# One VectorE instruction for the row sums of an attention head: a column sum that transposes its input, in place of a 32 by 32 transposition and a sum

## The chip, the cores and the metric

The kernel runs on one core of a Trainium2 chip. The metric is the device time of one execution in microseconds (us), the median of several runs. The engines of the core are TensorE (PE in the profile; its weight loads are PEld), VectorE (DVE), ScalarE (ACT), GpSimd (POOL) and SyncE (SP), which issues the transfers.

## The reference

Block-causal attention for 8 batches of 8 heads (576 positions, 64 columns a head, blocks of 64), and behind it a gated MLP on all 4608 positions:

```python
scores = scale * np.matmul(q, k.transpose(0, 1, 3, 2))      # q, k, v: (8, 8, 576, 64)
mask = block_i >= block_j                                   # blocks of 64 positions
scores = np.where(mask, scores, -1000000000.0)
scores = scores - np.max(scores, axis=-1, keepdims=True)
attn = np.exp(scores)
attn = attn / (np.sum(attn, axis=-1, keepdims=True) + 1e-09)
x = np.matmul(attn, v)          # heads side by side: (4608, 512)
a = x @ w1                      # (512, 1024)
b = x @ w2
h = a * b @ w3                  # (1024, 1024)
out = h @ w_out                 # (1024, 512)
```

The change lies in `np.sum(attn, axis=-1)`.

## The kernel before, in words

The work is staged by pairs of heads, 32 of them (8 batches of 4 pairs), numbered n; j is the head of a pair. The scores are held transposed, keys on the 128 partitions (five chunks of 128 keys, the last of 64) and queries along the columns, so that the exponentials can go into the product with the values as they are. The sum over a row of the attention is then a sum over partitions and chunks.

The first four pairs run while the weights come in, and take their row sums in another way (a column of ones in the values; `take_early`). The change does not touch them. From the fifth pair on (about 170 us) each head goes as follows:

- `s_tile` (L235): products of q and k, each in two passes (`hi` and `lo` parts), into one of two PSUM tiles `s`. ScalarE takes the exponential twice, once in full precision into `p`, or into `rsum` for the first chunk (L250), and once rounded into `ph` (L251). VectorE makes the low part `pl` as the difference (L253). GpSimd adds the chunks of `p` into `rsum` (L256), a tile of 128 partitions by 576 queries.
- `pv` (L291): products of `ph` and `pl` with the values, into the PSUM tile `x`.
- `sums` (step R of the plan): `rsum` is transposed in blocks of 32 by 32 into `tr` (L304), and then each 32 columns of `tr` are added up (L305). The result, 18 columns a head, goes into `part`. Each of its numbers is the sum over one group of 32 partitions for one query.
- `take` (step N): ScalarE copies half of `x` to `xlow` (L323), VectorE adds the other half (L324).
- `total` (step T, once for both heads of a pair): a small product `tot` (L309) adds the four groups of partitions; VectorE adds 1e-9 (L311). `norm` takes the reciprocal (L327), spreads it by a transposition into `rb` (L329) and multiplies (L330). `finish_x` rounds to `xh` on ScalarE (L339) and makes the low part `xl` on GpSimd (L340).

For the next pair, the parts of q and k are prepared meanwhile: `hi` casts on VectorE (L160) with differences on GpSimd (L209, L212), `vs` for the values (cast on ScalarE, difference L225 on GpSimd), and the row maxima `m`: products `mx` (L182), maxima on VectorE (L186, L188), a transposition `mt` on TensorE (L190) and a copy on ScalarE (L192).

The MLP of the batch before is cut into small steps (F in the plan) that stand between those of the attention: products `ab` (L388) with copy `a` on ScalarE (L393), the gate `g` on VectorE (L395), `gh` on ScalarE (L396) and `gl` on GpSimd (L397), then products `o` (L404) with a copy (L408). After the last pair the MLP of the last batch runs alone.

The order of the work is set by a plan written out by hand, one letter a step, for the first and the second head of a pair:

```python
PLAN = (
    "B F B F S F S B F F S S F F F S M M V F V V V F R F F V Q N",
    "M A S S A F F S F M M S F F F S M A M V V V F V F F V N Q F R T M F F",
)
```

TensorE's order is this order as written. Every engine works through its own queue in order. A tile pool puts in the waits between engines.

Of the kernel before, what the change touches and what calls it, by code (L numbers as in the profile page):

```python
# [7 lines left out]
F32 = mybir.dt.float32  # L8
# [4 lines left out]
ALU = mybir.AluOpType  # L13
AX = mybir.AxisListType
PSUM = bass.MemoryType.PSUM

P = 128
B, H, S, D = 8, 8, 576, 64
BLK = 64
NB = S // BLK  # L20
NPAIR = H // 2
# [4 lines left out]
NF = DF // P  # L26
HALF = S // 2
RAW = 2 * S + 640
EARLY = NPAIR  # pairs whose work is spread over more engines while the weights come in
SCALE = 0.125  # L30
BIG = 8.0e9

# Columns of a head's probabilities (keys on partitions): a chunk of 128 keys
# takes the queries that may see it; zeros keep every product 256 columns wide.
PC = [128, 704, 1152, 1536, 1920]
PW = 1984
QLO = [0, 128, 256, 384, 512]
# The same without zeros, less the first query.
PE = [0, 448, 768, 960, 1024]


# Order of a head's steps, for the first and the second head of a pair.
PLAN = (
    "B F B F S F S B F F S S F F F S M M V F V V V F R F F V Q N",
    "M A S S A F F S F M M S F F F S M A M V V V F V F F V N Q F R T M F F",
)
# The same for the pairs before the first product of the MLP, while the weights come in.
EARLY_PLAN = (
    "M S S S C S C C C C M S V V B C M M V A V M V M Q B M A B M N",
    "S C C S A S S C S C V V V V V Q N T",  # L50
)
# Steps of the first pair with the MLP beside it that leave the MLP's place empty.
DELAY = 3
# Whether ScalarE makes the roundings of (q and k, q, k, k for the maxima, q for the maxima, v).
CAST = (0, 0, 1, 1, 1, 1)


# [1 line left out]
def block_causal_attention__then__gated_mlp_kernel(ctx, tc, qkv, consts, ident_in, w1, w2, w3t, wout, out_t):  # L59
    nc = tc.nc  # L60
# [4 lines left out]
    work = ctx.enter_context(tc.tile_pool(name="work", bufs=1))  # L65
# [6 lines left out]
    both = cpool.tile([P, 2 * P], F32, name="ident")  # L72
# [2 lines left out]
    w1l = cpool.tile([P, NC, DF], F32R, name="w1l")  # L75
    wh = cpool.tile([P, NF, DM], F32R, name="wh")
    wl = cpool.tile([P, NF, DM], F32R, name="wl")
    # Per head of a pair: (q, k) with high parts on the head's own half of the
    # partitions and q high, k low on the other; and (q low, k high) on the own
    # half with the rows that shift and mask the scores on the other.  # L80
    hi = [cpool.tile([P, 2, S], F32R, name=f"hi{j}") for j in range(2)]
    lo = [cpool.tile([P, 2, S], F32R, name=f"lo{j}") for j in range(2)]
    w2h = cpool.tile([P, NC, DF], F32R, name="w2h")
    w2l = cpool.tile([P, NC, DF], F32R, name="w2l")
    # Queries of both heads of a pair, block by block on a diagonal.
    qd = cpool.tile([P, NB, P], BF16, name="qd")
    own = [slice(0, D), slice(D, P)]
    oth = [slice(D, P), slice(0, D)]
# [12 lines left out]
    for j in range(2):  # L101
        nc.vector.tensor_copy(lo[j][oth[j]], cst[0:D, 0 : 2 * S].rearrange("p (t s) -> p t s", t=2))
    nc.gpsimd.memset(qd, 0.0)
    # Tiles of the time while the weights come in, and those that take their bytes.
    tl = {}

    def open_early(pool):
# [3 lines left out]
    def open_late():  # L111
        pool = ctx.enter_context(tc.tile_pool(name="late", bufs=1, reuse_waits="tile"))
        tl["late"] = pool
        tl["ph"] = pool.tile([P, PW], F32R, name="ph")
        tl["sum"] = pool.tile([P, S], F32, name="rsum")
        tl["pl"] = pool.tile([P, PW], F32R, name="pl")
        # Values: high part on the columns of the head's own half, low part on the other.
        tl["vs"] = [pool.tile([P, 5, P], F32R, name=f"vs{j}") for j in range(2)]
        for t in (tl["ph"], tl["pl"]):
            for a, b in ((0, PC[0]), (PC[2] + 320, PC[3]), (PC[3] + 192, PC[4])):  # L120
                nc.gpsimd.memset(t[:, a:b].bitcast(F32), 0.0)
        tl["gh"] = pool.tile([P, NF, HALF], F32R, name="gh")
        tl["gl"] = pool.tile([P, NF, HALF], F32R, name="gl")

    def load_w(dst, src, k):
        """512 columns of float64 words (low, high), as float32.

        Magnitudes below float32's smallest normal become zero.
        """
        t = tl["early"].tile([P, 1024], F32, tag="wraw", name="wraw", bufs=5)  # L130
        u = tl["early"].tile([P, 512], F32, tag="wbits", name="wbits", bufs=6)
        wide = t.bitcast(I32)
        nc.sync.dma_start(out=wide.rearrange("p (k w) -> p k w", k=k), in_=src)
        wide = wide.rearrange("p (c two) -> p c two", two=2)
        low, high = wide[:, :, 0], wide[:, :, 1]
        bits = u.bitcast(I32)
        V = nc.vector
        nc.scalar.activation(u, high.bitcast(F32), AF.Abs)
        V.tensor_scalar(out=u, in0=u, scalar1=2.0**-15, scalar2=None, op0=ALU.max)
        V.tensor_scalar(out=bits, in0=bits, scalar1=3, scalar2=0x3FFFFFF8, op0=ALU.logical_shift_left, op1=ALU.bitwise_and)  # L140
        V.scalar_tensor_tensor(out=bits, in0=high, scalar=-0x40000000, in1=bits, op0=ALU.bitwise_and, op1=ALU.bitwise_or)  # L141
        if dst is None:
            dst = u.unsqueeze(1)
        V.scalar_tensor_tensor(out=dst.bitcast(I32), in0=low.rearrange("p (k w) -> p k w", k=k), scalar=29,
                               in1=bits.rearrange("p (k w) -> p k w", k=k), op0=ALU.logical_shift_right, op1=ALU.bitwise_or)
        return u
# [115 lines left out]
        [(2, 256, 576, 256)],  # L262
        [(3, 320, 576, 384), (4, 512, 576, 512)],
    ]
    # (chunk, first column of the probabilities, width, first column in PSUM)
    PV = [(0, 0, 256, 256), (0, PC[0] + 128, 448, 512), (1, PC[1], 448, 512), (2, PC[2], 320, 640),
          (3, PC[3] - 64, 256, 704), (4, PC[4] - 192, 256, 704)]

# [30 lines left out]
    x_of = {}  # L299

    def sums(n, j, part):
        """Sums over the keys: 32 by 32 transposes, then over the groups of 32 partitions."""
        tr = work.tile([P, S], F32, tag="tr", name=f"tr{n}_{j}")
        nc.vector.transpose(tr, tl["sum"])  # L304
        nc.vector.reduce_sum(part[:, j, :], tr.rearrange("p (b c) -> p b c", c=32), axis=AX.X)  # L305

    def total(n, part, rr):
        tot = ps_q.tile([P, 512], F32, tag="psq", name=f"tot{n}")
# [117 lines left out]
    weights = gen_w(wp)  # L426

    def pair(n):
        """The attention of a pair of heads, with what the plan places between its steps."""
        early = n < EARLY  # L430
        x32 = work.tile([P, S], F32, tag="x32", name=f"x32_{n}")
        rr = work.tile([P, S // 32], F32, tag="rr", name=f"rr{n}")
        part = None if early else work.tile([P, 2, S // 32], F32, tag="part", name=f"part{n}")
        last = n + 1 == NN
        masks = iter(()) if last else shift_mask(n + 1)
        own_qk = prep_qk(n, 1)
        next_qk = iter(()) if last else prep_qk(n + 1, 0)
        for j in range(2):
            xps = ps_x.tile([P, 1024], F32, tag="psx", name=f"x{n}_{j}")
            p_early = wp.tile([P, 1600], F32, tag="pe", name=f"pe{n}_{j}") if early else None  # L440
            tiles = iter(S_TILES)
            pvs = (pv_early if early else pv)(n, j, xps, p_early)
            delay = DELAY if n == NPAIR and j == 0 else 0
            for step in (EARLY_PLAN if early else PLAN)[j].split():
                if step == "C":
                    fill(weights, 1)
                    continue
                with tc.high_priority(offset=0) if early else nullcontext():
                    if step == "S":
                        s_tile(n, j, next(tiles), p_early)  # L450
                    elif step == "F":
                        if delay:
                            delay -= 1
                        else:
                            fill(mlp, 1)
                    elif step == "M":
                        fill(masks, 1)
                    elif step == "A":
                        fill(next_qk, 1)
                    elif step == "B":  # L460
                        fill(own_qk, 1)
                    elif step == "V":
                        fill(pvs, 1)
                    elif step == "R":
                        sums(n, j, part)
                    elif step == "N" and early:
                        take_early(n, j, xps, x32, rr)
                    elif step == "N":
                        take(n, j, xps, x32)
                    elif step == "T":  # L470
                        if not early:
                            total(n, part, rr)
                        norm(n, x32, rr)
                        finish_x(n, x32)
                    elif step == "Q" and not last:
                        if n + 1 != NPAIR:
                            prep_v(n + 1, j)
                        if j == 1 and n + 2 < NN:
                            load(n + 2)
# [5 lines left out]
    open_late()  # L485
    for j in range(2):
        prep_v(NPAIR, j)
    # Products of the gated MLP stand between those of the attention, which wait for other engines.
    ctx.enter_context(tc.manual_schedule(engines={mybir.EngineType.PE}))
    mlp = (None for b in range(B - 1) for _ in gen_moe(b))  # L490
    for n in range(NPAIR, NN):
# [52 lines left out]
```

## Time and profile before

| what | value |
|---|---|
| median of 3 runs | 1069.15 us (1067.49 to 1069.55) |
| span of the profiled execution | 1066.6 us, 18267 instructions |
| the profiled execution's time beside its span | not given apart; the median of the runs lies 2.55 us above the span |
| TensorE busy | 986.9 us (93%) |
| VectorE busy | 810.3 us (76%), 1432 instructions |
| ScalarE busy | 594.9 us (56%) |
| GpSimd busy | 601.4 us (56%) |
| mean granted TensorE clock | 0.982 |

The profile is one execution, with times from the start of the span. Matmuls are pipelined and their ends are modelled, so that the busy time of TensorE says less than the distance from one start to the next. In a row of a timeline the first number is the start, the second how long it took, both in us; a bracket at its end gives how long the engine had been idle before it and what ended that. The letters L and a number are a line of the kernel.

### The profile page before, as it was taken

The numbers are of one execution on the slowest core, as the hardware profiler recorded it, in microseconds if no ns is written. First come the engines' busy times: TensorE is split into PE (matmuls) and PEld (weight loads), VectorE is DVE, ScalarE is ACT, GpSimd is POOL, SyncE is SP. The second block draws the span as 40 slices with busy tenths as digits, with TensorE's granted clock in tenths as the row PEclk, the third lists the DMA queues.
The fourth block names the chain that finished last, engine by engine and source line by source line (L and its number), as shares of the span: only waits on it lengthen the run. The fifth ranks groups of instructions, "written<-read, shape, count | busy, mean of one in ns | idle before, by whom it ended". The sixth has DMA issues, their size and how long they took to land.

```text
span 1066.6 us, 18267 instructions
## 1 busy us (share of the span) xinstructions
PE 986.9 (93%) x6624; PEld 892.7 (84%) x6624; DVE 810.3 (76%) x1432; ACT 594.9 (56%) x1505; POOL 601.4 (56%) x631
## 2 busy tenths in 40 slices
PE   3789778999999999999999999999999999999998
PEld 1444347999998989999999989899999999899998
DVE  7999997878787887778787888877787878886100
ACT  4646566656665656556565656565565656554221
POOL 3324367656575666666565756666665657564211
PEclk9889889999999999999999999999999999999999
DMA  6665421111111001111111110111111111000000
GB/s 214 202 194 191 140 73 36 35 58 36 58 35 54 18 34 47 41 52 36 58 36 58 36 47 19 39 47 42 52 36 58 35 59 36 22 3 18 7 24 23
DMA packets 27196, 61.52 MB, mean 58 GB/s; under 512 B 3361, under 2 KB 19873, under 8 KB 27105
## 3 DMA queue, kind: packets, MB, share of 16 engines
q1 hardware_dynamic: 27104, 60.35, 17.0%
q8 instruction: 52, 0.85, 0.3%
q14 instruction: 40, 0.32, 0.1%
HBM read 50.76 MB, written 9.44 MB: 56 GB/s over the span
## 4 chain that ended last, share of the span: by engine, by line
PE 47%; DVE 34%; ACT 11%; issue 6%; DMA 1%; POOL 1%; ACTq 0%; DVEq 0%; SPq 0%; POOLq 0%
PE ab L388 21%; PE o L404 12%; DVE pl L253 6%; PE s L235 6%; DVE m L186 4%; DVE hi L160 3%; DVE part L305 3%; DVE tr L304 3%; ACT ph L251 3%; DVE g L395 2%; PE x L291 2%; ACT p L250 2%; PE mx L182 2%; PE w L365 2%; DVE wbits L141 2%
## 5 line engine op out<-in xcount | busy, mean ns | idle before, releaser
L256 POOL TENSOR_TENSOR rsum<-rsum,p 128x448 f32<-128x448 f32 x224 | 176.7, 789 | 124.1 <-ACT p L250 116.6
L253 DVE TENSOR_TENSOR pl<-p,ph 128x448 fp32r<-128x448 f32 x168 | 149.1, 901 | 62.2 <-ACT ph L251 61.3
L397 POOL TENSOR_TENSOR gl<-g,gh 128x288 fp32r<-128x288 f32 x128 | 107.5, 840 | 138.0 <-ACT gh L396 135.6
L396 ACT CAST gh<-g 128x288 fp32r<-128x288 f32 x128 | 55.5, 433 | 228.2 <-DVE g L395 228.2
L235 PE MATMUL s<-hi 128*128 128x288 f32 (+4 forms) x384 | 127.8, 344 | 29.0 <-ACT ph L251 21.4
L388 PE MATMUL ab<-xh,w2h 128*128 128x288 f32 x512 | 153.3, 300 | 0.1
L404 PE MATMUL o<-gh,wh 128*128 128x288 f32 x512 | 152.1, 297 | 0.0
L388 PE MATMUL ab<-xh,w1h 128*128 128x288 f32 x512 | 150.9, 295 | 1.1 <-ACT xh L339 1.1
L388 PE MATMUL ab<-xl,w1h 128*128 128x288 f32 x512 | 151.0, 295 | 0.5 <-POOL xl L340 0.5
L388 PE MATMUL ab<-xh,w2l 128*128 128x288 f32 x512 | 150.9, 295 | 0.0
L388 PE MATMUL ab<-xh,w1l 128*128 128x288 f32 x512 | 150.9, 295 | 0.0
L388 PE MATMUL ab<-xl,w2h 128*128 128x288 f32 x512 | 150.9, 295 | 0.0
L404 PE MATMUL o<-gh,wl 128*128 128x288 f32 x512 | 150.8, 295 | 0.0
L404 PE MATMUL o<-gl,wh 128*128 128x288 f32 x512 | 150.7, 294 | 0.0
L186 DVE TENSOR_REDUCE m<-mx 128x1 f32<-128x512 f32 (+6 forms) x320 | 128.1, 446 | 5.0 <-PE mx L182 3.2
L251 ACT ACTIVATE ph<-s 128x288 fp32r<-128x288 f32 x336 | 131.3, 393 | 0.0
L209 POOL TENSOR_TENSOR hi<-raw,hi 64x576 fp32r<-64x576 f32 x64 | 93.7, 1464 | 43.2 <-ACT hi L160 17.8
L291 PE MATMUL x<-ph,vs 128*128 128x256 f32 x336 | 111.6, 340 | 0.1
L250 ACT ACTIVATE p<-s 128x448 f32<-128x448 f32 x224 | 85.4, 381 | 44.6 <-PE s L235 44.3
L235 PE MATMUL s<-lo 128*128 128x288 f32 (+4 forms) x384 | 107.0, 307 | 2.2 <-DMA lo<-ms 1.2
L235 PEld LDWEIGHTS s<-hi 128*128 128x128 f32 (+1 forms) x384 | 70.9, 185 | 45.5 <-ACT ph L251 28.0
L395 DVE TENSOR_TENSOR g<-ab,a 128x288 f32<-128x288 f32 x128 | 57.4, 448 | 66.4 <-PE ab L388 65.5
(77 smaller groups left out, 2558.7 us busy)
## 6 DMA issues: line engine op xcount, KB each, us to landing
raw<-in_qkv SPq DMA_DIRECT2D x32, 896.0 KB
out_t<-o SPq DMA_DIRECT2D x64, 144.0 KB
wraw<-in_w3t SPq DMA_DIRECT2D x16, 512.0 KB
wraw<-in_w SPq DMA_DIRECT2D x16, 512.0 KB
wraw<-in_wout SPq DMA_DIRECT2D x8, 512.0 KB
lo<-ms SPq DMA_DIRECT2D x64, 2.2 KB
cst<-in_consts SPq DMA_DIRECT2D x1, 288.0 KB
ident<-in_ident SPq DMA_DIRECT2D x1, 128.0 KB
```

Source lines behind the costliest of these rows:

```text
L186: nc.vector.reduce_max(m[:, col : col + 1], sc, axis=AX.X)
L209: nc.gpsimd.tensor_tensor(out=hi[j][x, 1, :], in0=rqk[o, 1, :], in1=hi[j][o, 1, :], op=ALU.subtract)
L235: nc.tensor.matmul(t[ks, at : at + q1 - q0], src[:, 1, kr], src[:, 0, q0:q1], start=(s == 0), stop=(s == 1))
L250: nc.scalar.activation(p32, t[ks, at : at + w], AF.Exp, scale=SCALE)
L251: nc.scalar.activation(ph[ks, o : o + w], t[ks, at : at + w], AF.Exp, scale=SCALE)
L253: nc.vector.tensor_tensor(out=low, in0=p32, in1=ph[ks, o : o + w], op=ALU.subtract)
L256: nc.gpsimd.tensor_tensor(out=r, in0=r, in1=p32, op=ALU.add)
L291: nc.tensor.matmul(xps[:, to : to + w], v[:, c, :], pr[:, a : a + w], start=(u < 2 and s == 0), stop=(u in (0, len(PV) - 1) and s == len(p ...
L388: nc.tensor.matmul(t[:, 0:HALF], l[:, c, fs], r, start=(c == 0 and s == 0), stop=(c == NC - 1 and s == 2))
L395: nc.vector.tensor_tensor(out=g32, in0=acc[1][:, 0:HALF], in1=a32, op=ALU.mult)
L397: nc.gpsimd.tensor_tensor(out=gl[:, f, :], in0=g32, in1=gh[:, f, :], op=ALU.subtract)
L404: nc.tensor.matmul(t[:, 0:HALF], l[:, f, es], r[:, f, :], start=(f == 0 and s == 0), stop=(f == NF - 1 and s == 2))
```

## The change

`sums` loses the transposition and the tile `tr`. The sum over each 32 columns reads `rsum` itself and is told to transpose its input in blocks of 32 by 32 (`apply_transpose=True`).

```diff
     def sums(n, j, part):
-        """Sums over the keys: 32 by 32 transposes, then over the groups of 32 partitions."""
-        tr = work.tile([P, S], F32, tag="tr", name=f"tr{n}_{j}")
-        nc.vector.transpose(tr, tl["sum"])
-        nc.vector.reduce_sum(part[:, j, :], tr.rearrange("p (b c) -> p b c", c=32), axis=AX.X)
+
+        blocks = tl["sum"].rearrange("p (b c) -> p b c", c=32)
+        nc.vector.tensor_reduce(part[:, j, :], blocks, axis=AX.X, op=ALU.add, apply_transpose=True)
```

The rest of the change takes out comments, so that lines behind L304 have a number less by one. The order of every other instruction on every engine is as before; on VectorE the new one stands where the transposition stood. Two places in VectorE's queue show it. The first is the sums of the first head of pair 6, `hi_84` being the cast for the next pair's first head, `m` the next pair's maxima and `g` the MLP's gate; before:

```order
L186 TENSOR_REDUCE m_2020<-mx_0_2021 128x1 [waits PE_49]
L304 STREAM_TRANSPOSE tr_0_2047<-rsum 128x576 [waits DVE_49,Pool_49]
L160 CAST hi_84<-raw_1854 64x576
L305 TENSOR_REDUCE part_1905<-tr_0_2047 128x18 [waits DVE_49]
L395 TENSOR_TENSOR g_2058<-ab,a_2056 128x288 [waits PE_49,Activation_49]
L186 TENSOR_REDUCE m_2020<-mx_1_2076 128x1 [waits PE_49]
```

After the change the cast is followed by the gate at once:

```order
L186 TENSOR_REDUCE m_2012<-mx_0_2013 128x1 [waits PE_49]
L304 TENSOR_REDUCE part_1897<-rsum 128x18 [waits Pool_49]
L160 CAST hi_84<-raw_1848 64x576
L394 TENSOR_TENSOR g_2048<-ab,a_2046 128x288 [waits PE_49,Activation_49]
L186 TENSOR_REDUCE m_2012<-mx_1_2066 128x1 [waits PE_49]
```

So `part` comes ahead of the cast instead of behind it, and `g` moves up one place. The second is the sums of the second head of pair 5, with `tot` and the normalisation behind them; before:

```order
L304 STREAM_TRANSPOSE tr_1_1862<-rsum 128x576 [waits DVE_49,Pool_49]
L188 TENSOR_TENSOR m_1649<-m_1649 128x1 [waits DVE_49]
L160 CAST hi_85<-raw_1475 64x576
L305 TENSOR_REDUCE part_1530<-tr_1_1862 128x18 [waits DVE_49]
L324 TENSOR_TENSOR x_5_1528<-x_1_1704,xlow_1_1849 64x576 [waits Activation_49]
L311 TENSOR_SCALAR rr_1529<-tot_1865 64x18 [waits PE_49]
```

After it:

```order
L304 TENSOR_REDUCE part_1526<-rsum 128x18 [waits Pool_49]
L188 TENSOR_TENSOR m_1645<-m_1645 128x1 [waits DVE_49]
L160 CAST hi_85<-raw_1473 64x576
L323 TENSOR_TENSOR x_5_1524<-x_1_1698,xlow_1_1843 64x576 [waits Activation_49]
L310 TENSOR_SCALAR rr_1525<-tot_1857 64x18 [waits PE_49]
```

Here `part` moves ahead of m and the cast, and x stands directly behind the cast.

## The prediction

> **What bounds the kernel now.** I read the stretches first, then the waits of TensorE, then the two tiles that the change touches, and last the timeline of two neighbouring pairs. The table by stretches cuts the span where the attention with the MLP beside it begins (170 us) and ends (985 us); its columns are the busy time of each engine with instruction counts, then the granted clock.
>
> ```profile
> core 0: us, PE busy (x) PEld busy (x) DVE busy (x) ACT busy (x) POOL busy (x), PEclk, DMA share, GB/s
> 170.00:985.00 815.00, 781.97 (x5643) 745.56 (x5643) 649.90 (x1160) 476.35 (x1271) 514.29 (x553) 1.00 0.12 40
> 985.00:1066.60 81.60, 78.42 (x592) 78.19 (x590) 8.09 (x18) 17.68 (x43) 14.48 (x18) 0.99 0.06 19
> ```
>
> TensorE is busy 96% of the middle stretch at full clock, VectorE 80%. All the changed instructions lie in that stretch, so VectorE time counts only where TensorE waits for it, directly or through another engine. The waits of TensorE there (us in total, times, longest):
>
> ```profile
> PE s L235 <- ACT ph L251: 21.4, 27, 0.8
> PE tot L309 <- DVE part L305: 7.7, 13, 0.6
> PE x L291 <- DVE pl L253: 3.6, 14, 0.3
> ```
>
> One is named after the changed instruction itself (L305), once in every second pair. The largest, 27 times, is named after ScalarE; the timeline shows what stands behind it. First the two instructions in question, from the view of the tile between them (min/median/max ns):
>
> ```profile
> L304 DVE STREAM_TRANSPOSE tr<-rsum x56: 765/768/778, 176.9 to 979.5; 128x576 f32<-128x576 f32 x56
> L305 DVE TENSOR_REDUCE part<-tr x56: 728/753/754, 178.5 to 980.4; 128x18 f32<-128x576 f32 x56
> ```
>
> They take 43 + 42 us of VectorE in 56 heads. Both are flat whatever GpSimd does beside them.
>
> **The first place: sums of a pair's first head (27 TensorE waits).** VectorE's, ScalarE's and TensorE's timelines in one pair (start, us):
>
> ```profile
> 411.24 0.69 DVE L186 TENSOR_REDUCE m<-mx 128x1 f32<-128x512 f32 x1
> 411.85 0.77 DVE L304 STREAM_TRANSPOSE tr<-rsum 128x576 f32<-128x576 f32 x1
> 412.64 0.70 DVE L160 CAST hi<-raw 64x576 fp32r<-64x576 f32 x1
> 413.38 0.75 DVE L305 TENSOR_REDUCE part<-tr 128x18 f32<-128x576 f32 x1
> 414.05 0.45 DVE L395 TENSOR_TENSOR g<-ab,a 128x288 f32<-128x288 f32 x1
> ```
> ```profile
> 414.53 0.43 ACT L396 CAST gh<-g 128x288 fp32r<-128x288 f32 x1 [3.45 <-DVE g L395]
> 414.87 0.46 ACT L160 CAST vs<-raw 128x320 fp32r<-128x320 f32 x1
> 415.35 0.64 ACT L323 COPY xlow<-x 64x576 f32<-64x576 f32 x1
> 416.01 0.41 ACT L250 ACTIVATE rsum<-s 128x288 f32<-128x288 f32 x1
> 416.31 0.41 ACT L251 ACTIVATE ph<-s 128x288 fp32r<-128x288 f32 x1
> ```
> ```profile
> 412.41 0.29 PE L388 MATMUL ab<-xl,w2h 128*128 128x288 f32 x1
> 413.34 0.28 PE L291 MATMUL x<-ph,vs 128*128 128x256 f32 x1
> 415.55 0.29 PE L388 MATMUL ab<-xh,w2l 128*128 128x288 f32 x1
> 415.68 0.29 PE L388 MATMUL ab<-xl,w2h 128*128 128x288 f32 x1
> 416.77 0.47 PE L235 MATMUL s<-hi 128*128 128x448 f32 x1 [0.80 <-ACT ph L251]
> ```
>
> VectorE stands in a queue without gaps: transpose, a cast, the sum, then g. ScalarE had been idle 3.45 us for g, then works without gaps to the ph that TensorE waits for. So the sum (L305) is on the path that ends the wait. Matmuls start 0.13 apart (415.55, 415.68), so the late one was due at 415.81 and lost 416.77 - 415.81 = 0.96 us, more than the 0.80 of modelled idle.
>
> The new instruction stands where the transpose stood, and nothing stands where the sum stood. If it takes what the transpose took, g starts where the sum started, 413.38 instead of 414.05: 0.67 earlier. Nothing else holds g or its followers: the products it reads were issued by 412.41 + 0.29, and those that xlow reads ended by 413.34 + 0.28 = 413.62, against a new start of 415.35 - 0.67 = 414.68. The whole ScalarE row moves up 0.67 and the loss falls from 0.96 to 0.29. **Term 1: 27 x 0.67 = 18.1 us.**
>
> **The second place: sums of the second head.** Odd pairs first, where TensorE waits for `part` (13 times):
>
> ```profile
> 454.06 0.77 DVE L304 STREAM_TRANSPOSE tr<-rsum 128x576 f32<-128x576 f32 x1
> 454.75 1.08 DVE L188 TENSOR_TENSOR m<-m 128x1 f32<-128x1 f32 x1
> 455.85 0.46 DVE L160 CAST hi<-raw 64x576 fp32r<-64x576 f32 x1
> 456.34 0.75 DVE L305 TENSOR_REDUCE part<-tr 128x18 f32<-128x576 f32 x1
> 457.12 0.76 DVE L324 TENSOR_TENSOR x<-x,xlow 64x576 f32<-64x576 f32 x1
> ```
> ```profile
> 456.26 0.29 PE L404 MATMUL o<-gl,wh 128*128 128x288 f32 x1
> ...
> 457.15 0.41 PE L309 MATMUL tot<-part,ident 128*128 128x36 f32 x2 [0.60 <-DVE part L305]
> ```
> ```profile
> 455.80 0.63 ACT L323 COPY xlow<-x 64x576 f32<-64x576 f32 x1 [0.68 <-PE x L291]
> ```
>
> Here `part` comes at 457.09; from one instruction in the transpose's place it comes at 454.83, before TensorE is due (456.26 + 0.13 = 456.39). The whole loss goes, 457.15 - 456.39 = 0.76. VectorE keeps up: x (L324) moves from 457.12 to when xlow ends, 456.43, a gain of 0.69, so that the normalisation behind it is no later against TensorE than now, to 0.07. **Term 2: 13 x 0.76 = 9.9 us.**
>
> In even pairs TensorE never waits for `part`, and VectorE gains nothing either:
>
> ```profile
> 425.87 0.73 DVE L305 TENSOR_REDUCE part<-tr 128x18 f32<-128x576 f32 x1
> 426.52 0.14 DVE L188 TENSOR_TENSOR m<-m 128x1 f32<-128x1 f32 x1
> 426.69 1.10 DVE L160 CAST hi<-raw 64x576 fp32r<-64x576 f32 x1
> ```
> ```profile
> 425.16 1.44 POOL L212 TENSOR_TENSOR lo<-raw,hi 64x576 fp32r<-64x576 f32 x1
> ...
> 454.38 1.44 POOL L212 TENSOR_TENSOR lo<-raw,hi 64x576 fp32r<-64x576 f32 x1
> ```
>
> The one-column m (L188) takes 0.14 here and 1.08 in the odd pair, where it begins inside GpSimd's L212 and ends with it (454.38 + 1.44 = 455.82). In the even pair `part` happens to cover L212 (to 426.60). Without it m starts inside L212 and still ends at 426.66: the 0.73 turns into blocking. [...] Without this blocking 0.73 of VectorE would come free in even pairs too, but no TensorE wait hangs on it, so **term 3 is 0**.
>
> Nothing is moved past another queue; GpSimd's, ScalarE's and SyncE's orders stand, and the tile `tr` merely loses two users per head. The new instruction waits on GpSimd's additions into rsum as the transpose did; behind it on VectorE are the cast and g. Before, that wait cost 0.3 us once. Some later VectorE instructions now wait for an earlier one of their own engine, long done in an engine that works in order: nothing, and a hundredth of a us each at most by the 0.02 to 0.04 between the rows above.
>
> **The price nobody has measured: the fused instruction.** No row shows it. It streams the same 576 columns, so less than 0.75 is excluded; both old jobs in a row make 0.77 + 0.75 = 1.52 the other end. I take 0.77: the two rows are alike, so a pass over 576 columns sets them, and one pass is what a transposing read needs if it feeds the adder. [...] No run here shows the combination.
>
> **Sum.** 18.1 + 9.9 = 28.0. The page gives the profiled execution's span, 1066.6, and no other time of it; the span becomes 1038.6. The median of the runs, 1069.15, lies 2.55 above it, which I carry along: 1069.15 - 28.0 = 1041.1, say 1041.
>
> **Rivals.**
> (a) The fused instruction takes both passes, 1.52. Then g starts as late as now (411.85 + 1.52 + 0.70 + gaps), term 1 is 0, but `part` still comes at 455.58, before 456.39, and term 2 stays: 1069.15 - 9.9 = 1059.3. For it: nothing in the trace shows a fused rate. Against: the equal rows.
> [...]
> (c) TensorE is the bound and other waits grow by what these lose (x behind pl, 14 times, is the likeliest): no change, 1069. [...] Against it: both waits end in the changed instructions, and everything behind them moves up together.
> (d) Slower: the fused instruction does not overlap filling, draining and adding in its 18 blocks. g moves by the duration less 1.44, term 2 holds until 2.33 (456.39 - 454.06), so it decides at 1.44 + 9.9/27 = 1.81. At three passes, 0.77 + 2 x 0.60 = 1.97 with 0.15 of each row taken as fixed, the first place loses 27 x 0.53 = 14.3 against 9.9: 1073.6.
>
> That the change does not do what it says is excluded by the instruction list: 56 VectorE instructions fewer.
>
> **How the numbers follow.** Forecast 1041: 0.58; (b) 1046: 0.14; (a) 1059, or between: 0.14; (c) 1069: 0.06; (d) 1074: 0.08. A gain beyond the forecast ends where all three TensorE waits above go: 27 x 0.96 + 9.9 + 3.6 = 39.4, 1030. The range 1030 to 1060 takes in that bound, (b) and (a), and leaves out (c) and (d), 0.14, and something for the size. Faster by over 0.2% (2.1 us, about what the spread of the three runs lets a measurement tell from no change): 0.58 + 0.14 + 0.14 = 0.86; within: 0.06; slower: 0.08.
>
> **What would show it.** One L304 reduction of about 0.77 in place of two rows; the wait for ph about 0.3 of lost time 27 times; no wait of tot for part; m (L188) near 0.8 in even pairs; two neighbouring pairs in 58.8 - 2.1 = 56.7 us. A duration over 1.4, or a wait of TensorE that is new, makes the prediction wrong.

## The result, and the profile after

The changed kernel takes 1035.7 us (median; 1035.29 to 1037.52) against 1068.75 before. The ratio is 0.9697, 95% interval 0.9685 to 0.9708: 33 us faster. Five more runs of it beside later experiments gave 1035.74 (0.970, 0.9687 to 0.9714). Its profiled span is 1033.5 against 1066.6.

The stretch of the attention after, in the columns of the table of before:

```profile
core 0: us, PE busy (x) PEld busy (x) DVE busy (x) ACT busy (x) POOL busy (x), PEclk, DMA share, GB/s
170.00:955.00 785.00, 777.74 (x5666) 748.27 (x5666) 617.57 (x1105) 476.68 (x1273) 519.52 (x555) 1.00 0.12 42
```

TensorE went from 96% to 99% busy there, at the same clock. VectorE is still far from full (79%). The new instruction, from the view of its tile:

```profile
L304 DVE TRANSPOSE_TENSOR_REDUCE part<-rsum x56: 768/769/780, 176.7 to 946.4; 128x18 f32<-128x576 f32 x56
```

It takes 0.769 us, what the transposition alone took (0.768). The adding is free. The waits of TensorE in the stretch:

```profile
PE x L291 <- DVE pl L253: 3.6, 14, 0.3
PE s L235 <- ACT ph L251: 0.7, 4, 0.2
```

The 21.4 us of waits for ph are down to 0.7 of modelled idle, the 7.7 us for `part` are gone, and the wait of x behind pl, which could have grown, is the same 3.6. Two neighbouring pairs take 56.3 us, where the prediction said 56.7 and the kernel before took 58.7 (mean distance of every second `tot` from 191 us on). The first place, on VectorE, ScalarE and TensorE:

```profile
401.74 0.77 DVE L304 TRANSPOSE_TENSOR_REDUCE part<-rsum 128x18 f32<-128x576 f32 x1
402.52 0.71 DVE L160 CAST hi<-raw 64x576 fp32r<-64x576 f32 x1
403.27 0.46 DVE L394 TENSOR_TENSOR g<-ab,a 128x288 f32<-128x288 f32 x1
```
```profile
403.76 0.43 ACT L395 CAST gh<-g 128x288 fp32r<-128x288 f32 x1 [2.78 <-DVE g L394]
...
405.55 0.40 ACT L251 ACTIVATE ph<-s 128x288 fp32r<-128x288 f32 x1
```
```profile
405.44 0.29 PE L387 MATMUL ab<-xh,w2l 128*128 128x288 f32 x1
405.58 0.29 PE L387 MATMUL ab<-xl,w2h 128*128 128x288 f32 x1
406.01 0.47 PE L235 MATMUL s<-hi 128*128 128x448 f32 x1
```

The matmul was due at 405.58 + 0.13 = 405.71 and came at 406.01: 0.30 lost, where the prediction said 0.29. In odd pairs `tot` no longer waits:

```profile
444.43 0.30 PE L403 MATMUL o<-gl,wh 128*128 128x288 f32 x1
444.57 0.31 PE L308 MATMUL tot<-part,ident 128*128 128x36 f32 x2
```

What the prediction did not have is in even pairs, behind the second head's sums. VectorE and GpSimd after:

```profile
415.10 0.75 DVE L188 TENSOR_TENSOR m<-m 128x1 f32<-128x1 f32 x1
415.88 0.46 DVE L160 CAST hi<-raw 64x576 fp32r<-64x576 f32 x1
```
```profile
414.40 1.43 POOL L212 TENSOR_TENSOR lo<-raw,hi 64x576 fp32r<-64x576 f32 x1
415.91 1.09 POOL L396 TENSOR_TENSOR gl<-g,gh 128x288 fp32r<-128x288 f32 x1
```

m (L188) takes 0.75, held until L212 ends (m at 415.85, L212 at 415.83), as predicted. But the cast behind it now starts at 415.88, 0.03 before GpSimd's gl (415.91), and takes 0.46; before, gl started first (426.67 against 426.69) and the cast took 1.10:

```profile
426.67 0.80 POOL L397 TENSOR_TENSOR gl<-g,gh 128x288 fp32r<-128x288 f32 x1
```

Now gl is the one held, 1.09 instead of 0.80. So VectorE did come out ahead in even pairs, and a wait of TensorE hung on it. Before the change:

```profile
433.76 0.44 DVE L395 TENSOR_TENSOR g<-ab,a 128x288 f32<-128x288 f32 x1
```
```profile
433.90 0.31 PE L235 MATMUL s<-lo 128*128 128x320 f32 x1
434.26 0.40 PE L388 MATMUL ab<-xh,w2h 128*128 128x288 f32 x1
434.50 0.29 PE L388 MATMUL ab<-xh,w2l 128*128 128x288 f32 x1
```

and after:

```profile
423.11 0.31 PE L235 MATMUL s<-lo 128*128 128x320 f32 x1
423.26 0.29 PE L387 MATMUL ab<-xh,w2h 128*128 128x288 f32 x1
423.39 0.30 PE L387 MATMUL ab<-xh,w2l 128*128 128x288 f32 x1
```

The first product came 0.36 behind the one ahead of it where 0.15 is usual, the second 0.24 where 0.13 is: 0.32 lost in all, just behind a g that ended at 434.20. After the change the same starts are 0.15 and 0.13 apart. The critical path of before leads from the cast at 426.69 to this place without a gap over 0.2 us: over x, rr, rb, x, xh, rsum, ph, pl and g.

The place comes once in every two pairs, but the pair shown is the worst of them: counted in all 14, the loss is 0.07 to 0.32, 2.4 us together. And it is not the only one. The waits of the weight loads in the stretch, of before and of after, show a second wait in the same pairs, of x for ph, some 5 us later (of the lines that both lists have, x behind pl is left out: 9.3 and 9.4 us):

```profile
PEld s L235 <- ACT ph L251: 27.7, 27, 1.1
PEld tot L309 <- DVE part L305: 10.7, 13, 0.8
...
PEld x L291 <- ACT ph L251: 3.3, 14, 0.4
PEld ab L388 <- DVE g L395: 1.5, 7, 0.3
```
```profile
PEld s L235 <- ACT ph L251: 9.9, 27, 0.4
...
PEld x L291 <- ACT ph L251: 0.8, 5, 0.2
```

The gain can be added up from the distances between matmul starts in the whole stretch, less the usual distance for the width: 17.8 us at s behind ph (25.8 before, 8.0 after), 9.8 at `tot`, 1.4 at `mt` behind it (it came 0.24 after a late `tot`, 13 times, and comes 0.14 after one that is in time), 2.4 at ab behind g, 1.4 at x behind ph. That is 32.8 of the 33.05.

### The profile page after: what moved, and what is told of

It is laid out like the page before. It is cut to its first block, busy times and chain, and to the rows that moved or that the text cites. A ratio compares the mean times of both kernels' runs of the same rounds, so it can differ in the third digit from the quotient of the medians.

```text
span 1033.5 us, 18295 instructions
## 1 busy us (share of the span) xinstructions
PE 977.6 (95%) x6624; PEld 891.3 (86%) x6624; DVE 777.6 (75%) x1376; ACT 594.3 (58%) x1505; POOL 605.2 (59%) x631
## 4 chain that ended last, share of the span: by engine, by line
PE 53%; DVE 25%; ACT 12%; issue 7%; DMA 2%; POOL 1%; DVEq 0%; ACTq 0%; SPq 0%; POOLq 0%
PE ab L387 20%; PE o L403 17%; DVE pl L253 6%; PE s L235 6%; PE x L291 5%; DVE g L394 3%; ACT ph L251 3%; PE mx L182 3%; ACT xlow L322 2%; ACT p L250 2%; DVE wbits L141 2%; DVE m L186 2%; DVE wbits L139 2%; DVE hi L160 2%; PE w L364 1%
## 5 line engine op out<-in xcount | busy, mean ns | idle before, releaser
L396 POOL TENSOR_TENSOR gl<-g,gh 128x288 fp32r<-128x288 f32 x128 | 111.8, 873 | 120.3 <-ACT gh L395 118.9
L186 DVE TENSOR_REDUCE m<-mx 128x1 f32<-128x512 f32 (+6 forms) x320 | 128.6, 449 | 6.2 <-PE mx L182 2.6
L209 POOL TENSOR_TENSOR hi<-raw,hi 64x576 fp32r<-64x576 f32 x64 | 93.3, 1457 | 42.5 <-ACT hi L160 17.4
L253 DVE TENSOR_TENSOR pl<-rsum,ph 128x288 fp32r<-128x288 f32 x112 | 65.1, 582 | 48.4 <-ACT ph L251 44.6
```

The source lines that it names most:

```text
L186: nc.vector.reduce_max(m[:, col : col + 1], sc, axis=AX.X)
L209: nc.gpsimd.tensor_tensor(out=hi[j][x, 1, :], in0=rqk[o, 1, :], in1=hi[j][o, 1, :], op=ALU.subtract)
L253: nc.vector.tensor_tensor(out=low, in0=p32, in1=ph[ks, o : o + w], op=ALU.subtract)
L396: nc.gpsimd.tensor_tensor(out=gl[:, f, :], in0=g32, in1=gh[:, f, :], op=ALU.subtract)
```

## The experiments

Theory A is the recorded sum: 18.1 (first heads) + 9.9 (odd pairs' second heads), nothing in even pairs. Theory B adds the wait of ab for g in even pairs, 14 x 0.32 = 4.5 as if every place lost what the worst one does; ab and x together lose 3.8 by the count above. All compare with before on the same chip.

Where an expectation says who has the port, the traces show the turns alone: m or the cast of `hi`, started inside a GpSimd instruction, ends 0.01 to 0.32 behind it (m at 415.85 behind L212 at 415.83 after the change, the cast at 427.79 behind gl at 427.47 before it), and gl, started 0.03 behind the cast, takes 1.09 instead of 0.80. That a port is behind these turns was my assumption; no run shows it.

**The new instruction in first heads alone.**

```diff
     def sums(n, j, part):
+        if j == 0:
             (the transposing sum)
+            return
+        (the transposition and the sum of before)
```

> The one transposing instruction in a pair's first head only; the second head keeps the transposition and the sum apart. Theory A (the recorded sum): this is term 1 alone, 27 x 0.67 = 18.1 us, so 1068.75 - 18.1 = 1050.7; the wait for ph (PE s) loses about 0.3 each time instead of 0.96, the 13 waits of tot for part stay at 0.76 each. Theory B (term 3 of the recorded sum is not 0: in even pairs VectorE gains in the second head as well, which ends a wait of ab for g of about 0.3): the same here, since the second heads are as before, and the waits of ab for g stay. A rival, that any VectorE time saved counts alike: half of the whole gain of 33.1, 1052.2.

Measured: 1049.22 against 1068.4 (0.9819, 0.9801 to 0.9838), 19.2 us less. TensorE's waits:

```profile
PE tot L313 <- DVE part L309: 7.7, 13, 0.6
...
PE s L235 <- ACT ph L251: 0.8, 5, 0.2
```

The wait for ph is gone by itself, the one for `part` is untouched, and so are those of the weight loads for g (1.7) and for ph ahead of x (3.3). Term 1 stands.

**In second heads alone** (`if j == 1`, else as above).

> The one transposing instruction in a pair's second head only. Theory A (the recorded sum): term 2 alone, 13 x 0.76 = 9.9 us, 1058.9. Theory B: besides it the wait of ab for g in even pairs, 14 x 0.32 = 4.5 us, goes, because the cast behind m now gets hold of the port ahead of GpSimd's gl: 1054.3; the cast of 64x576 in even pairs takes 0.46 instead of 1.10, m (L188) 0.75 instead of 0.14. Both: the 27 waits for ph stay at 0.96. The rival, that VectorE time counts alike: 1052.2.

Measured: 1053.39 (0.9855, 0.984 to 0.987), 15.0 less (13.9 to 17.1 by the interval): near theory B's 14.4, not the 9.9 of the recorded sum. By the count above the second heads make 9.8 + 1.4 + 2.4 + 1.4 = 15.0, and in this run's trace the weight loads wait for g no more and for ph ahead of x only 0.7. The two halves add up to 34.2, the whole change gave 33. In an even pair:

```profile
305.43 0.74 DVE L188 TENSOR_TENSOR m<-m 128x1 f32<-128x1 f32 x1
306.21 0.46 DVE L160 CAST hi<-raw 64x576 fp32r<-64x576 f32 x1
```

The cast is short here too, while with the first heads alone it took 1.10 behind an m of 0.15.

**Turning that race round.** The change, with a tiny instruction behind m:

```diff
         nc.vector.tensor_tensor(out=m[:, 8:9], in0=m[:, 8:9], in1=m[:, 9:10], op=ALU.max)
+        if n > NPAIR:
+            spare = work.tile([P, 1], F32, tag="spare", name=f"spare{n}")
+            nc.vector.reduce_max(spare, m[:, 4:6], axis=AX.X)
```

> The change, with one more tiny VectorE instruction (maximum of two columns into a spare tile, 0.1 to 0.2 us) between m (L188) and the cast behind it, in the pairs beside the MLP. Theory B: m ends 0.06 before gl starts on GpSimd, the tiny instruction lets gl have the port first, the cast takes about 1.1 again instead of 0.46, in even pairs everything behind it is 0.4 to 0.6 later, and the wait of ab for g is back: 1035.7 + 14 x 0.32 = 1040.2. Theory A (nothing hangs on VectorE's time there): 1035.7, within 0.5.

Measured: 1041.53 (0.9745, 0.973 to 0.976), 5.8 above the change. VectorE and GpSimd in an even pair, then TensorE behind it:

```profile
416.61 0.75 DVE L188 TENSOR_TENSOR m<-m 128x1 f32<-128x1 f32 x1
417.28 0.14 DVE L191 TENSOR_REDUCE spare<-m 128x1 f32<-128x2 f32 x1
417.43 1.10 DVE L160 CAST hi<-raw 64x576 fp32r<-64x576 f32 x1
```
```profile
417.41 0.80 POOL L399 TENSOR_TENSOR gl<-g,gh 128x288 fp32r<-128x288 f32 x1
```
```profile
424.64 0.30 PE L238 MATMUL s<-lo 128*128 128x320 f32 x1
425.02 0.40 PE L390 MATMUL ab<-xh,w2h 128*128 128x288 f32 x1
425.25 0.29 PE L390 MATMUL ab<-xh,w2l 128*128 128x288 f32 x1
```

0.14 us on VectorE let gl start first (417.41 against 417.43). The cast is back at 1.10 in all 14 even pairs, and the 0.38 and 0.23 between starts on TensorE are back. This pair is again the worst: over the whole stretch ab behind g loses 1.6 and x behind ph 1.1 more than after the change, 2.7 of the 5.8, while s behind ph loses 0.7 less. Another 2.6 is spread evenly: the products of the MLP that wait for nothing start 0.1334 apart on average in this profile and 0.1327 in that of the change, 3610 times. Why is open, and so is the rest; the race itself is worth 2.7 here.

**The same VectorE time as before, but the result early.** Behind the new instruction a sum of the same tile that nobody reads:

```diff
         nc.vector.tensor_reduce(part[:, j, :], blocks, axis=AX.X, op=ALU.add, apply_transpose=True)
+        spare = work.tile([P, S // 32], F32, tag="spare", name=f"spare{n}_{j}")
+        nc.vector.reduce_sum(spare, blocks, axis=AX.X)
```

> The one transposing instruction in both heads, and behind it a second sum of the same tile into a spare tile that nobody reads, 0.75 us: VectorE has as much to do as before, but part comes as early as after the change. Theory A: term 1 is gone and term 2 stays, 1035.7 + 18.1 = 1053.8, or by the recorded rival (a) 1059.3 less what term 3 holds. Theory B: the spare sum also covers GpSimd's L212 in even pairs, so that m takes 0.14 again, the cast loses the port to gl and the wait of ab for g is back: 1035.7 + 18.1 + 4.5 = 1058.3. If not VectorE's time but the earlier part were what counts, 1036.

Measured: 1079.62 (1.0094, 1.008 to 1.0109). Both theories missed by over 20 us: this is slower than before the change. TensorE's largest wait, and the first place on VectorE and GpSimd:

```profile
PE s L235 <- ACT ph L251: 36.9, 27, 1.7
```
```profile
415.68 0.77 DVE L304 TRANSPOSE_TENSOR_REDUCE part<-rsum 128x18 f32<-128x576 f32 x1
416.37 0.71 DVE L306 TENSOR_REDUCE spare<-rsum 128x18 f32<-128x576 f32 x1
417.10 1.57 DVE L160 CAST hi<-raw 64x576 fp32r<-64x576 f32 x1
418.69 0.46 DVE L396 TENSOR_TENSOR g<-ab,a 128x288 f32<-128x288 f32 x1
```
```profile
416.93 1.42 POOL L212 TENSOR_TENSOR lo<-raw,hi 64x576 fp32r<-64x576 f32 x1
```

The spare sum stands ahead of the cast, where the old sum stood behind it. So the cast comes at 417.10, behind the start of L212 (416.93), and is held to its end at 418.35: 0.71 of extra work became 1.48 of delay for g (415.68 to 418.69 from the new instruction to g, against 401.74 to 403.27). 27 x 1.48 = 40, with the 3.8 of the even pairs 43.8; the kernel is 43.9 slower than the change. The distances on TensorE agree: 33.3 more at s behind ph and 6.1 at ab behind g in the first places, 3.9 in the even pairs.

**The spare sum behind the cast.** It reads `part` spread over 32 columns, which places it where the old sum stood:

```diff
+        nc.vector.reduce_sum(spare, part[:, j, :].unsqueeze(2).broadcast_to([P, S // 32, 32]), axis=AX.X)
```

> As the kernel with the spare sum (1079.6), but the spare sum reads part, spread over 32 columns, and stands where the old sum stood: behind the cast in first heads and in odd pairs' second heads, ahead of m in even pairs. VectorE's work is that of before again, and part still comes early. If the spare sum ahead of the cast cost so much because it let GpSimd's L212 have the port first (the cast took 1.57), the cast takes 0.7 again here and the time is 1035.7 + 18.1 for the wait for ph + 4.5 to 5.8 for the wait of ab for g = 1058 to 1060. If it was the spare instruction as such, 1079.6 again.

Measured: 1057.0 (0.9895, 0.9881 to 0.9908), a us below the range given, and 22.6 below the kernel with the spare sum ahead of the cast. The cast takes 0.68:

```profile
409.16 0.68 DVE L160 CAST hi<-raw 64x576 fp32r<-64x576 f32 x1
409.87 0.75 DVE L306 TENSOR_REDUCE spare<-part 128x18 f32<-128x576 f32 x1
410.54 0.45 DVE L396 TENSOR_TENSOR g<-ab,a 128x288 f32<-128x288 f32 x1
```

This is the change with VectorE's time given back: what is left of the gain, 11.4 us, is the earlier `part` (9.8 at `tot` and 1.4 at `mt` behind it).

**A short spare sum ahead of the cast** (`blocks[:, 13:18]`, 160 columns).

> As the kernel with the spare sum ahead of the cast (1079.6), but the spare sum reads the last 160 columns of rsum only, about 0.3 us by the reductions of 128 and 192 columns (0.27 and 0.35). If the cost lies in who gets the port: the cast then starts at about 402.8 in the place shown of the changed kernel, still ahead of GpSimd's L212 (403.00), is held by L209 as before and ends where it ended; m in second heads is held by L212 as before: 1035.7, within 0.2%. If VectorE's time ahead of g is what counts, 27 x 0.3 = 8 us more, 1044; if it goes in proportion to the long spare sum, 44 x 0.3 / 0.71 = 19 us more, 1054.

Measured: 1035.4 (0.969, 0.9676 to 0.9703), no change. The spare sum takes 0.28, and it costs nothing:

```profile
403.26 0.28 DVE L306 TENSOR_REDUCE spare<-rsum 128x5 f32<-128x160 f32 x1
403.55 0.49 DVE L160 CAST hi<-raw 64x576 fp32r<-64x576 f32 x1
```
```profile
402.31 1.42 POOL L209 TENSOR_TENSOR hi<-raw,hi 64x576 fp32r<-64x576 f32 x1
403.80 1.53 POOL L212 TENSOR_TENSOR lo<-raw,hi 64x576 fp32r<-64x576 f32 x1
```

The cast starts later but is ahead of L212 and shorter (0.49, not 0.71), as part of its time had been waiting for L209: it ends 0.31 behind L209 here (404.04 and 403.73) as in the changed kernel (403.23 and 402.92). So the same work ahead of the cast costs nothing at 0.28 and 44 us at 0.71.

**m as a reduction.**

```diff
-        nc.vector.tensor_tensor(out=m[:, 8:9], in0=m[:, 8:9], in1=m[:, 9:10], op=ALU.max)
+        if n > NPAIR:
+            nc.vector.reduce_max(m[:, 8:9], m[:, 8:10], axis=AX.X)
+        else:
             (the maximum of before)
```

> The change, with m's last maximum (L188) made by a reduction over two neighbouring columns (one input) instead of a maximum of two inputs, in the pairs beside the MLP. If VectorE shares a port with GpSimd that two inputs or a cast need and a reduction does not: L188 takes about 0.15 in all pairs instead of 0.75 and 1.08, and the cast behind it takes the blocking over, starting earlier and ending where it ended, with about 1.0 to 1.4 of duration; the time stays at 1035.7 within 0.2%. If L188 was slow for another reason (m's own data, the queue), the cast starts and ends 0.6 to 0.9 earlier and keeps its 0.46.

Measured: 1034.18 (0.9682, 0.9669 to 0.9696), the change's time within 0.2%. The reduction is not held (0.112 to 0.135 in all 27); the blocking goes to the cast, which starts inside GpSimd's `lo` and ends 0.31 behind it (415.76 and 415.45). In odd pairs the cast takes 1.23 to 1.24, inside the range given; in even pairs it takes 0.88, less than that, and ends 2.08 behind the start of the sums where it was 2.27 (414.07 to 416.34):

```profile
414.71 0.14 DVE L189 TENSOR_REDUCE m<-m 128x1 f32<-128x2 f32 x1
414.88 0.88 DVE L160 CAST hi<-raw 64x576 fp32r<-64x576 f32 x1
```
```profile
414.01 1.44 POOL L215 TENSOR_TENSOR lo<-raw,hi 64x576 fp32r<-64x576 f32 x1
```

**What still held ph.** The cast of vs for the next pair's first head moves from step Q of the first head to a step P behind the second head's first scores:

```diff
-    "... V V V F R F F V Q N",
-    "M A S S A F F S F ...",
+    "... V V V F R F F V N",
+    "M A S S A F F S P F ...",
...
+                    elif step == "P" and not last:
+                        prep_v(n + 1, 0)
```

> The change, and the cast of the next pair's values for the first head (vs on ScalarE, 0.46) taken from ahead of xlow to behind the second ph of the next head. If the 0.28 that TensorE still loses 27 times at the wait for ph hangs on ScalarE's row gh, vs, xlow, rsum, ph, then ph comes 0.46 earlier, that wait goes, and the time is 1035.7 - 27 x 0.28 = 1028.1. If something else holds it there, 1035.7.

Measured: 1030.18 (0.9645, 0.9632 to 0.9659), 5.5 less than the change where 7.6 were expected. TensorE's wait for ph ahead of s is gone from the list, and with it the 8.0 us of distances; on the weight loads a wait for ph ahead of x has come up to 2.8 us from 0.8, which takes 2.0 back:

```profile
PEld x L291 <- ACT ph L251: 2.8, 13, 0.3
```

**Both together.**

> The change with both edits that were not slower: the cast of vs behind the second ph (1030.2) and m's last maximum as a reduction (1034.2). If the two are apart, 1030.2 - 1.5 = 1028.7; if the 1.5 of the reduction was scatter between runs, 1030.2.

Measured: 1029.82 (0.9642, 0.9629 to 0.9655): nothing that can be told from 1030.18. Moving vs is the version that beats both kernels. The 1.5 of m's reduction does not add to it; by the expectation that makes it scatter, though a gain that the move of vs uses up is not excluded.

## Why the prediction was right, and where not

- **The fused price** (0.77, from two equal rows): 0.769. Right.
- **Term 1**, 18.1: 19.2 by itself (17.3 to 21.3 by its interval), 17.8 by the distances, with 0.27 to 0.33 left at each of the 27 places where 0.29 was forecast. The step that carried it was to see that a wait named after ScalarE's ph hung on a VectorE sum, four ScalarE instructions earlier.
- **Term 2**, 9.9: the wait for `part` is gone to the last, 9.8. The term left out the small product `mt` behind it, which a late `tot` put off by another 0.10 each time: 11.2 in all, and the kernel in which only the early `part` is left gained 11.4. With the even pairs' share, second heads made 15.0.
- **Term 3**, 0: the step that failed. m was held as forecast, 0.75. But I let the cast behind it stay where it was, "still ends at 426.66", and did not ask which of the two queues would then start first; and I wrote that "no TensorE wait hangs on it" from the list of the matmuls' waits, where these losses mostly do not show, since the modelled ends of matmuls cover them. Two waits hung on it, of ab for g and of x for ph; the distance between starts shows them, and so does the list of the weight loads (1.5 and 3.3 us). Their measured size is 2.4 + 1.4 = 3.8; 2.7 came back with the race turned round. I first priced this at 14 x 0.32 = 4.5 from the worst pair, without x behind ph and `mt`; that 18.1 + 9.9 + 4.5 = 32.5 came so near 33.05 was luck. Of the miss of 5 us, 3.8 belong to term 3 and 1.3 to term 2, and term 1 was 0.3 too large: 17.8 + 11.2 + 3.8 = 32.8.
- **Rivals (a) and (d)**: their prices were wrong, though the fused instruction did not put them to the test. I let the delay of g grow with the instruction's length. The spare sum made 1.48 of the pair, nearly (a)'s 1.52, and gave 1079.6, not 1059.3: past the start of L212 (416.93) the cast was held to its end (1.57, where it took 0.71) and the price jumped. The short one shows that the first 0.28 cost nothing. The deciding length lies between 0.77 + 0.28 = 1.05 and 0.77 + 0.71 = 1.48, as far as a spare sum can stand for a longer instruction, and not at the 1.81 of the text. The 0.60 a pass in (d), a row less 0.15 taken as fixed, was my estimate, and no run shows such a pass of the fused instruction; plain reductions of before (L186) took 0.209 for 64 columns and 0.686 for 512, 1.06 ns a column and 0.14 fixed.
- **Rival (b)**, 1046 in the chances, had GpSimd's gl and vs move up less than the rest and pl stay 0.20 behind for it, 27 x 0.20 = 5.4 us. No run shows the 0.20. Counted from the start of the sums, gl and vs did move up less (gl from 3.26 to 2.75, vs from 4.03 to 3.51, against ph from 4.46 to 3.81), but pl moved up the same 0.65 as ph and no TensorE wait came of it: pl starts 0.44 behind the start of ph in the first place as before (416.31 to 416.75, now 405.55 to 405.99), 0.30 is lost, and x behind pl is the same 3.6. Fallen. **(c)** fell with the times.

## What to carry to other kernels

A busy engine (TensorE at 96%) can still owe its last per cents to a slower chain: take the largest wait, walk back through the engines that work without gaps to it, and a saving anywhere in that chain counts in full until the wait is used up (here 17.8 us by the distances, for the 27 x 0.67 = 18.1 that were saved). List the losses by the distance between matmul starts, not by modelled idle alone, and count them at every place: one pair can be the worst of them (0.32 here, where the mean was 0.17). Where VectorE and GpSimd take turns, an instruction's price can be decided by whether it lets the other queue start first: here an edit of 0.14 us came with 5.8 us, of which 2.7 could be traced to the turned order, one of 0.28 cost nothing, one of 0.71 forty-four.

## What the hardware showed

The transposing sum over 128 x 576 float32 costs what the transposition costs (0.769 against 0.768): the adding behind it took no time of its own. What it costs per column no run here shows, since only 576 columns ran. On VectorE the maximum m, of two inputs, and the cast of `hi` took turns with GpSimd's instructions, the one that started first going ahead for a whole instruction: the traces of before, of the change and of these edits agree (m at 0.14 to 0.15 or held up to 1.09, the cast at 0.46 or held up to 1.57), and m's maximum as a reduction was never held (0.112 to 0.135 in 27).
